# Loading feed-forward weights as fp32 through the hardware queue with a GpSimd cast, and reordering the first and last steps of an attention and feed-forward kernel

## The chip, the cores and the metric

The kernel runs on one core of one Trainium2 chip. The metric is the device time of one execution in microseconds (us). Thirteen executions of the kernel before gave a median of 504.83 us, from 499.0 to 512.78 us.

## The reference

The inputs are `q`, `k` and `v` with 8 batches, 8 heads, 576 rows and a head size of 64, in fp32, and four fp32 weight matrices.

```
scores = q @ k.T / 8                      # per batch and head, 576 x 576
thresh = max(scores, axis=-1) - tau       # tau = 0.02
attn   = softmax(scores where scores >= thresh, else -1e9)
x      = (attn @ v), heads side by side   # 4608 x 512
h      = max(x @ w1, x @ w2, x @ w3)      # 4608 x 768, w1, w2, w3 are 512 x 768
out    = h @ w_out                        # w_out is 768 x 512
```

## The kernel before, in words

**Quads and steps.** Four heads of one batch are a quad; there are 16 quads, two to a batch. A quad takes 9 steps. A step computes the scores of 128 rows of two heads (two tiles of 128x576 in PSUM), their row maxima (VectorE, `nm` and `unused`), two exponentials (ScalarE, `z`), for some tiles a masked multiply (VectorE, `z`), and then two reciprocals (`rs`) and the normalized bf16 tile `P` (GpSimd). A DMA transpose on SyncE's queue turns `P` into a part of `ptq`. There are 144 steps, and each has exactly one `rs` instruction, so that the starts of those are a clock of the steps. Everything is issued through `_Ordered`, whose line 62 is the line that the profile shows for nearly all instructions.

**Other work in the steps.** Each step has two slots for a piece of other work: a transposition of the next quad's `q` or `k` on TensorE (`tp`), a product of `ptq` with `vb` (`o`, evacuated into `xt`), a product of the hidden layer (`hid`, PSUM tile `ph`, for one block `f` of 128 hidden columns and one of the weights), or a product of the output (`po`). The dictionary `plan` has fixed slots for the first two kinds (`TS`, `PA`, `PB`, counted in half steps from the quad's start). Pieces of the feed-forward network wait in the list `todo`, and a free slot takes one; from slot 18*14+`ED` on it takes two. Once both quads of a batch have their `o` products, `o_step` appends the batch's 18 hidden pieces and its output pieces to `todo`. What is left after the last step is done by `rest`.

**Halves.** With two column runs per piece, `hid` issues matmuls of 64 rows that use the upper and the lower half of the array at once, in two rounds that `halves` separates by a gate (a no-op that waits for the first round). When a step has exactly two pieces, `issued` interleaves them in the order of `ARRAY`, so that one piece's second round comes after the other's first. With more than two pieces, or one, a piece's rounds follow each other directly. The last batch is done in two parts with one run of 256 and one of 320 columns, with matmuls of 128 rows.

**Weights.** `weight_loads` makes nine DMAs on GpSimd's queue that cast from fp32 to bf16 on the way: three of 256 columns (`f` 0 and 1), three of 512 columns (`f` 2 to 5), and three pieces of `wo`. They are issued after the steps in `WL`. The hidden pieces of the first batch begin at step 25.

**Order and buffers.** On each engine the instructions of a step follow `ORDER`, where M is the maxima, E the first exponentials, N and K the numerators, R the reciprocal and `P`, and V and A the evacuations of the two pieces. Four buffers hold `z`, six hold `P`, and the loads of `q`, `k` and `v` of a quad have two each and are on SyncE's queue (lines 154 to 174), as are the transposes (line 302) and the stores of the output.

Of the kernel before, what the change touches and what calls it, by code (L numbers as in the profile page):

```python
# [30 lines left out]
ORDER = "V0 A0 R0 K0 V1 M0 M1 A1 N0 K1 N1 E0 E1"  # L31
LAG = dict(M=0, E=0, N=1, K=1)
LATE = 0
ED = 28
WF = (0, 256, 768)
WO = (0, 2, 4, 6)
WL = (14, 16, 18, 24, 26, 28, 31, 33, 35)
LQ = 0
LV = 0
NC = 3  # L40
TS = (9, 11, 13, 15)
PA = 12
PB = 14
# [30 lines left out]
def kernel(  # L74
# [22 lines left out]
    nc = tc.nc  # L97
# [7 lines left out]
    NF = DF // 128  # L105
# [6 lines left out]
    wts = [one.tile([128, 4, DF], BF16, name=f"w{i}") for i in range(3)]  # L112
    wo = one.tile([128, NF, DM], BF16, name="wo")

    def weight_loads():

        for f0, f1 in zip(WF, WF[1:]):
            for w, t in zip((moe_w1, moe_w2, moe_w3), wts):
                yield lambda w=w, t=t, f0=f0, f1=f1: pool.dma_start(
                    out=t[:, :, f0:f1], in_=w[:, f0:f1].rearrange("(ko p) f -> p ko f", p=128))  # L120
        for f0, f1 in zip(WO, WO[1:]):
            yield lambda f0=f0, f1=f1: pool.dma_start(
                out=wo[:, f0:f1, :], in_=moe_w_out[f0 * 128:f1 * 128, :].rearrange("(ko p) m -> p ko m", p=128))
# [240 lines left out]
    def ffn(b, xt, hT, runs, chunks):  # L364


        st = {}
        nr, n = len(runs), runs[0][1] - runs[0][0]

        def hid(f, wi):  # L370
            my = {}

            def start():
                if wi == 0:
                    st["hm"] = hp_.tile([128, nr, n], BF16, name="hm", bufs=3)
                my["hm"], my["ps"] = st["hm"], slot("ph")

            def operands(kc, a):
                c0, c1 = runs[a]
                return (my["ps"][:, a * 512:a * 512 + n],  # L380
                        lambda rows: wts[wi][rows, kc, f * 128:(f + 1) * 128],
                        lambda rows: xt[rows, kc, c0:c1])

            def first():
                start()
                if nr == 1:
                    for kc in range(4):
                        o, w, m = operands(kc, 0)
                        tensor.matmul(o, w(slice(0, 128)), m(slice(0, 128)), start=(kc == 0), stop=(kc == 3))
                else:  # L390
                    my["h"] = halves([[operands(kc, a) for kc in range(4)] for a in range(2)])
                    my["h"][0]()

            def done():
                hm = my["hm"]
                pv = my["ps"].rearrange("p (a u) -> p a u", a=2)[:, :nr, :n]
                if wi == 0:
                    scalar.activation(out=hm, in_=pv, func=AF.Copy)
                else:
                    dst = hm if wi == 1 else \  # L400
                        hT[:, f, runs[0][0]:runs[-1][1]].rearrange("p (a u) -> p a u", a=nr)
                    vector.tensor_tensor(out=dst, in0=pv, in1=hm, op=OP.max)
            return [_Piece(first, (lambda: my["h"][1]()) if nr == 2 else None, done, "V" if wi else "A")]

        rows_out = out[b * S:(b + 1) * S, :].rearrange("(p c) m -> p c m", c=9)

        def outp(c):

            my = {}

            def first():
                my["ps"] = ps = slot("po")
                my["h"] = halves([[(ps[:, 512 * a:512 * a + 512],
                                    lambda rows, a=a, f=f: hT[rows, f, (c + a) * 128:(c + a) * 128 + 128],
                                    lambda rows, f=f: wo[rows, f, :]) for f in range(NF)] for a in range(2)])
                my["h"][0]()

            def done():
                for a in range(2):
                    ob = hp_.tile([128, DM], F32, name="ob", bufs=4)  # L420
                    scalar.activation(out=ob, in_=my["ps"][:, 512 * a:512 * a + 512], func=AF.Copy)
                    nc.sync.dma_start(out=rows_out[:, (0, 2, 1, 3)[c + a]:8:4], in_=ob)
            return [_Piece(first), _Piece(lambda: my["h"][1](), None, done, "A")]

        def ninth():

            my = {}

            def first():
                my["ps"] = ps = slot("po")  # L430
                for f in range(NF):
                    for x in range(2):
                        tensor.matmul(ps[64 * x:64 * x + 64, :256], hT[:, f, 512:S], wo[:, f, 256 * x:256 * x + 256],
                                      start=(f == 0), stop=(f == NF - 1))

            def done():
                ob = hp_.tile([128, DM // 2], F32, name="obr", bufs=2)
                scalar.activation(out=ob, in_=my["ps"][:, :256], func=AF.Copy)
                for x in range(2):
# [3 lines left out]
        return ([pc for f in range(NF) for wi in range(3) for pc in hid(f, wi)],  # L443
                [outp(c) if c < 4 else ninth() for c in chunks])


# [55 lines left out]
    def others(n):  # L502

        ps = []
        for when in (2 * n, 2 * n + 1):
            if when in plan:
                for fn in plan[when]:
                    ps.extend(fn())
            else:
                for _ in range(2 if when >= e + ED else 1):  # L510
                    if todo:
                        ps.append(todo.pop(0))
        return ps

# [27 lines left out]
        return out  # L542

    wl = list(weight_loads())
    for t in vrs:
        for x in range(2):
            vector.memset(t[64 - 64 * x:128 - 64 * x, 2 * x:2 * x + 2, :], 0.0)
# [11 lines left out]
    def step(n, ps):  # L559

        if n + 1 < len(steps):
            g, idx = steps[n + 1]
            c = dict(g=g, idx=idx, z=zz.tile([128, W], F32, name="z"), sm=small.tile([128, 2], F32, name="sm"))

            def scored(r):
                c[r] = scores(Ls[g], idx, r)
            dones = issued(ps, (lambda: scored(0), lambda: scored(1)))
        else:
            c = None
            dones = issued(ps)  # L570
        hist.append(c)
        for what in ORDER.split():
            k, r = what[0], int(what[1])
            if k in "AV":
                if r < len(dones) and dones[r][0] == k:
                    dones[r][1]()
                continue
            x = hist[-1 - LAG.get(k, 0)] if len(hist) > LAG.get(k, 0) else None
            if k == "M" and x:
                x["bias", r] = maximum(x["g"], x["idx"], r, x[r])  # L580
            elif k == "E" and x:
                exponents(x["g"], x["idx"], r, x["z"], x[r], x["bias", r])
            elif k in "NK" and x and masked(x["g"], x["idx"], r) == (k == "K"):
                numerators(x["g"], x["idx"], r, x["z"], x["sm"])
                if r == 1:
                    norm.append(x)
            elif k == "R" and len(norm) > LATE:
                x = norm.pop(0)
                normalized(Ls[x["g"]], x["idx"], x["z"], x["sm"])

    step(-1, [])
    for n, (g, idx) in enumerate(steps):
# [9 lines left out]
        if n % 9 == NC and n // 9 + 1 < NQ:  # L602
            cast_v(Ls[n // 9 + 1])
        step(n, others(n))
        if wl and n in WL:
            wl.pop(0)()
    for _ in range(max(LAG.values()) - 1):
        step(len(steps), [])
    for x in norm:
        normalized(Ls[x["g"]], x["idx"], x["z"], x["sm"])  # L610

    def rest(p):
        for _, done in issued([p]):
            done()
    while todo:
        rest(todo.pop(0))
    for pr in range(2):
        for p in o_step(z_, pr, 2):
            rest(p)
    for p in todo + held:  # L620
        rest(p)
# [1 line left out]
_INS = ['q', 'k', 'v', 'tau', 'moe_w1', 'moe_w2', 'moe_w3', 'moe_w_out']  # L623
_OUTS = [((4608, 512), 'float32')]
# [30 lines left out]
```

## Time and profile before

| | |
|---|---|
| median of 13 executions | 504.83 us |
| profiled execution, its own time | 505.38 us |
| span of its instructions | 503.6 us |
| mean granted TensorE clock | 0.968 |
| TensorE busy | 457.8 us (91%) |
| VectorE busy | 401.9 us (80%) |
| ScalarE busy | 394.3 us (78%) |
| GpSimd busy | 301.3 us (60%) |
| DMA, mean rate | 167 GB/s |

The profiled execution is one execution: its span starts with the first instruction and ends with the last. Busy times count an engine's instructions without its waits. A line of the timeline gives start and length in us, engine, operation, tiles, and, in brackets, the idle time before it and what ended that. The clock row gives the granted TensorE clock in tenths, in 40 slices of 12.6 us.

### The profile page before, as it was taken

What the parts mean: (1) busy time and instruction counts of PE and PEld (TensorE: products, weight loads), DVE (VectorE), ACT (ScalarE), POOL (GpSimd) and SP (SyncE); (2) the same over time, 40 slices, a digit from 0 to 9 for tenths busy, and PEclk for the clock granted to TensorE, in tenths of its full rate; (3) what the DMA queues carried; (4) which work ended last, traced back from release to release, by engine and by line L of the source; (5) the groups of instructions that cost most, each with busy time, mean ns of one, the idle gap of its engine ahead of it and who ended that gap; (6) DMA issues with size and microseconds to landing.
All of it is one profiled execution on the core that took longest, in us unless ns stands there. A gap on an engine that the chain in (4) does not pass through costs nothing.

```text
span 503.6 us, 14001 instructions
## 1 busy us (share of the span) xinstructions
PE 457.8 (91%) x5188; PEld 307.4 (61%) x5188; DVE 401.9 (80%) x996; ACT 394.3 (78%) x814; POOL 301.3 (60%) x413
## 2 busy tenths in 40 slices
PE   7778779389899999999999999999999989999995
PEld 6334347257457675866667675867567665665772
DVE  4998969379499997999798987999799997876450
ACT  4998968279598889889898889889898888864522
POOL 3899877357475747566575757575665876333200
PEclk9897959799899999999999999999999999999999
DMA  7999999989999798978799898979699547842602
GB/s 222 252 216 177 179 233 143 182 167 196 199 194 204 148 191 176 221 167 192 138 213 184 147 189 191 215 156 186 135 237 160 102 83 162 133 85 54 160 12 96
DMA packets 211701, 84.30 MB, mean 167 GB/s; under 512 B 186288, under 2 KB 199344, under 8 KB 211632
## 3 DMA queue, kind: packets, MB, share of 16 engines
q1 hardware_dynamic: 207088, 79.66, 78.8%
q0 software_dynamic: 3984, 3.15, 5.0%
q8 instruction: 41, 0.67, 0.6%
q10 hardware_dynamic: 560, 0.59, 0.4%
q14 instruction: 28, 0.23, 0.2%
HBM read 34.60 MB, written 9.44 MB: 87 GB/s over the span
## 4 chain that ended last, share of the span: by engine, by line
PE 56%; DVE 16%; ACT 12%; DMA 8%; issue 6%; POOL 2%; SPq 0%; ACTq 0%; DVEq 0%; POOLq 0%
PE ph L62 22%; PE sc L62 19%; ACT z L62 9%; PE po L62 9%; DVE unused L62 6%; PE o L62 6%; DVE z L62 4%; DMA w<-in_moe_w_dram 3%; DMA ptq<-P 2%; DVE nm L62 2%; DMA wo<-in_moe_w_out_dram 2%; PE tp L62 2%; ACT ob L62 1%; POOL P L62 1%; DMA qm<-in_q_dram 1%
## 5 line engine op out<-in xcount | busy, mean ns | idle before, releaser
L62 POOL TENSOR_SCALAR P<-z,rs 128x576 bf16<-128x576 f32 x288 | 214.8, 758 | 154.6 <-DVE rs L62 129.1
L62 ACT ACTIVATE z<-sc,nm 128x576 f32<-128x576 f32 x288 | 198.0, 741 | 46.8 <-DVE unused L62 27.1
L62 PE MATMUL sc<-kt,qs 64*128 64x256 f32 (+2 forms) x640 | 190.3, 435 | 10.9 <-ACT z L62 9.7
L62 PE MATMUL sc<-kt,qt 64*128 64x320 f32 (+2 forms) x640 | 190.8, 446 | 8.8 <-ACT z L62 7.8
L62 PE MATMUL ph<-xt,w 64*128 64x288 bf16 (+2 forms) x2160 | 164.5, 285 | 9.7 <-DMA w<-in_moe_w_dram 9.0
L62 DVE TENSOR_SCALAR_CACHE_REDUCE unused<-sc 128x576 bf16<-128x576 f32 x189 | 138.5, 749 | 36.1 <-PE sc L62 35.8
L62 PEld LDWEIGHTS <-w 64*128 64x128 bf16 (+1 forms) x2160 | 127.4, 95 | 42.9 <-issue 12.3
L62 ACT ACTIVATE z<-z 128x576 f32<-128x576 f32 x189 | 129.5, 692 | 0.0
L62 PEld LDWEIGHTS sc<-kt,qs 64*128 64x128 f32 (+1 forms) x640 | 90.2, 181 | 41.7 <-ACT z L62 33.9
L62 PEld LDWEIGHTS sc<-kt,qt 64*128 64x128 f32 (+1 forms) x640 | 91.1, 181 | 32.9 <-ACT z L62 29.3
L62 DVE SCALAR_TENSOR_TENSOR z<-z 128x576 f32<-128x576 f32 x99 | 88.6, 895 | 0.0
L62 DVE TENSOR_REDUCE nm<-sc 128x1 f32<-128x576 f32 x99 | 74.5, 752 | 0.4 <-PE sc L62 0.3
L62 POOL COPY qs<-qt 64x640 f32<-64x640 f32 (+1 forms) x62 | 53.5, 862 | 15.2 <-ACT qt L62 12.1
L62 DVE TENSOR_TENSOR hm<-ph,hm 128x576 bf16<-128x576 f32 (+2 forms) x54 | 37.3, 691 | 29.1 <-PE ph L62 21.9
L62 PE MATMUL po<-wo,hT 64*128 64x512 bf16 (+1 forms) x480 | 54.1, 363 | 2.9 <-DMA wo<-in_moe_w_out_dram 1.9
L62 ACT ACTIVATE hm<-ph 128x576 bf16<-128x576 f32 (+2 forms) x54 | 32.2, 597 | 26.6 <-PE ph L62 26.6
L62 PEld LDWEIGHTS <-hT 64*128 64x128 bf16 (+1 forms) x480 | 26.8, 98 | 26.4 <-issue 8.5
L62 PE MATMUL o<-ptq,vb 128*64 128x64 bf16 (+2 forms) x544 | 41.4, 291 | 1.7 <-DMA ptq<-P 1.7
L62 DVE TENSOR_TENSOR hT<-ph,hm 128x576 bf16<-128x576 f32 (+2 forms) x54 | 37.1, 687 | 5.6 <-PE ph L62 3.9
L62 ACT ACTIVATION_READ_ACCUMULATOR z<-z 128x1 f32 x189 | 39.7, 210 | 0.0
L62 PEld LDWEIGHTS <-vb 128*64 128x64 bf16 x544 | 22.4, 113 | 24.1 <-issue 16.1
L62 DVE RECIPROCAL rs<-sm 128x2 f32<-128x2 f32 x144 | 22.9, 159 | 7.3 <-ACT z L62 2.2
(30 smaller groups left out, 239.9 us busy)
## 6 DMA issues: line engine op xcount, KB each, us to landing
vm<-in_v_dram SPq DMA_DIRECT2D x64, 128.0 KB, 2.9
out_dram<-ob SPq DMA_DIRECT2D x32, 256.0 KB, 2.7
qm<-in_q_dram SPq DMA_DIRECT2D x15, 512.0 KB, 4.4
km<-in_k_dram SPq DMA_DIRECT2D x15, 512.0 KB, 5.8
ptq<-P SPq DMA_TRANSPOSE x144, 3.8
w<-in_moe_w_dram POOLq DMA_DIRECT2D x3, 512.0 KB, 12.6
qm<-in_q_dram SPq DMA_DIRECT2D x16, 64.0 KB, 3.3
vr<-in_v_dram SPq DMA_DIRECT2D x32, 32.0 KB, 2.5
```

What stands on the lines that cost most here:

```text
L62: ins = fn(*a, **kw)
```

## The change

The weights are loaded as fp32 by SyncE's queue in twelve pieces of 512 KB into a buffer `stage` (two buffers), each issued after a step in the new `WL` and turned into bf16 by a GpSimd copy `WC` = 3 steps later. In the first 34 steps the order of work is `ORDER0`, in which the reciprocal and `P` come last instead of near the front, and one more tile may wait for them. The `o` products of the first three quads come two slots (one step) later. The `v` casts of a quad move two steps later (`NC`). In the last batch two hidden products share a PSUM slot and use the halves too. No slot takes two pieces any more (`ED` = 40 lies beyond the last slot), and `rest` issues its pieces in pairs.

```diff
+ORDER0 = "A0 V0 A1 V1 M0 M1 N0 N1 E0 E1 K0 K1 R0"
+N0 = 34
+GE = 3
+PA0 = 14
+PB0 = 16
-ED = 28
-WL = (14, 16, 18, 24, 26, 28, 31, 33, 35)
+ED = 40
+HOLD = 0
+WL = (11, 13, 15, 18, 20, 22, 24, 26, 28, 30, 31, 32)
+WC = 3
-NC = 3
+NC = 5
...
+    stage = ctx.enter_context(tc.tile_pool(name="stage", bufs=2))
...
-        for f0, f1 in zip(WF, WF[1:]):
-            for w, t in zip((moe_w1, moe_w2, moe_w3), wts):
-                yield lambda w=w, t=t, f0=f0, f1=f1: pool.dma_start(
-                    out=t[:, :, f0:f1], in_=w[:, f0:f1].rearrange("(ko p) f -> p ko f", p=128))
+            def load():
+                my["t"] = stage.tile([128, 4 * 256], F32, name="stage")
+                nc.sync.dma_start(out=my["t"].rearrange("p (k f) -> p k f", k=src.shape[1]), in_=src)
+
+            def cast():
+                pool.tensor_copy(out=dst, in_=my["t"].rearrange("p (k f) -> p k f", k=src.shape[1]))
+            return load, cast
+
+        for f in range(0, NF, 2):
+            cols = slice(f * 128, f * 128 + 256)
             for w, t in zip((moe_w1, moe_w2, moe_w3), wts):
+                yield piece(t[:, :, cols], w[:, cols].rearrange("(ko p) f -> p ko f", p=128))
...
-        def hid(f, wi):
+        def hid(*fws):
...
-                if nr == 1:
-                    for kc in range(4):
-                        o, w, m = operands(kc, 0)
-                        tensor.matmul(o, w(slice(0, 128)), m(slice(0, 128)), start=(kc == 0), stop=(kc == 3))
...
+        fws = [(f, wi) for f in range(NF) for wi in range(3)]
+        return ([hid(*fws[x:x + 3 - nr]) for x in range(0, len(fws), 3 - nr)],
...
-        at(18 * g + 18 + PA, lambda g=g: o_step(g, 0))
-        at(18 * g + 18 + PB, lambda g=g: o_step(g, 1))
+        at(18 * g + 18 + (PA0 if g < GE else PA), lambda g=g: o_step(g, 0))
+        at(18 * g + 18 + (PB0 if g < GE else PB), lambda g=g: o_step(g, 1))
...
-        for what in ORDER.split():
+        for what in (ORDER if n >= N0 else ORDER0).split():
...
-            elif k == "R" and len(norm) > LATE:
+            elif k == "R" and len(norm) > (LATE if n >= N0 else 1):
...
-        if wl and n in WL:
-            wl.pop(0)()
+        if n in WL:
+            ahead, behind = wl.pop(0)
+            ahead()
+            casts[n + WC] = behind
+        if n in casts:
+            casts[n]()
...
-    def rest(p):
-        for _, done in issued([p]):
-            done()
+    def rest(ps):
+
+        while ps:
+            for _, done in issued([ps.pop(0) for _ in range(min(2, len(ps)))]):
+                if done:
+                    done()
```

More of the change, by code (lines that the diff above doesn't have):

```diff
@@ L33 @@
 LATE = 0
-ED = 28
-WF = (0, 256, 768)
-WO = (0, 2, 4, 6)
-WL = (14, 16, 18, 24, 26, 28, 31, 33, 35)
+ORDER0 = "A0 V0 A1 V1 M0 M1 N0 N1 E0 E1 K0 K1 R0"
[7 more added lines that the diff above has]
+WC = 3
 LQ = 0
 LV = 0
-NC = 3
+NC = 5
 TS = (9, 11, 13, 15)
@@ L113, with piece @@
     wo = one.tile([128, NF, DM], BF16, name="wo")
+    stage = ctx.enter_context(tc.tile_pool(name="stage", bufs=2))
     def weight_loads():
-        for f0, f1 in zip(WF, WF[1:]):
-            for w, t in zip((moe_w1, moe_w2, moe_w3), wts):
-                yield lambda w=w, t=t, f0=f0, f1=f1: pool.dma_start(
-                    out=t[:, :, f0:f1], in_=w[:, f0:f1].rearrange("(ko p) f -> p ko f", p=128))
-        for f0, f1 in zip(WO, WO[1:]):
-            yield lambda f0=f0, f1=f1: pool.dma_start(
-                out=wo[:, f0:f1, :], in_=moe_w_out[f0 * 128:f1 * 128, :].rearrange("(ko p) m -> p ko m", p=128))
+        def piece(dst, src):
+            my = {}
+            def load():
[6 more added lines that the diff above has]
+            cols = slice(f * 128, f * 128 + 256)
+            for w, t in zip((moe_w1, moe_w2, moe_w3), wts):
+                yield piece(t[:, :, cols], w[:, cols].rearrange("(ko p) f -> p ko f", p=128))
+        for f in range(0, NF, 2):
+            yield piece(wo[:, f:f + 2, :], moe_w_out[f * 128:f * 128 + 256, :].rearrange("(ko p) m -> p ko m", p=128))
     ld = ctx.enter_context(tc.tile_pool(name="ld", bufs=2))
@@ L368, in ffn @@
         nr, n = len(runs), runs[0][1] - runs[0][0]
-        def hid(f, wi):
+        def hid(*fws):
             my = {}
[L373 to L382, printed above, removed]
-            def first():
-                start()
-                if nr == 1:
-                    for kc in range(4):
-                        o, w, m = operands(kc, 0)
-                        tensor.matmul(o, w(slice(0, 128)), m(slice(0, 128)), start=(kc == 0), stop=(kc == 3))
-                else:
-                    my["h"] = halves([[operands(kc, a) for kc in range(4)] for a in range(2)])
-                    my["h"][0]()
-            def done():
[L395 to L403, printed above, removed]
@@ new lines, in hid @@
+            banks = [(f, wi, c) for f, wi in fws for c in runs]
+            def first():
+                my["ps"] = slot("ph")
+                my["h"] = halves([[(my["ps"][:, a * 512:a * 512 + n],
+                                    lambda rows, f=f, wi=wi, kc=kc: wts[wi][rows, kc, f * 128:(f + 1) * 128],
+                                    lambda rows, c=c, kc=kc: xt[rows, kc, c[0]:c[1]]) for kc in range(4)]
+                                  for a, (f, wi, c) in enumerate(banks)])
+                my["h"][0]()
@@ new lines, in done @@
+            def done():
+                pv = my["ps"].rearrange("p (a u) -> p a u", a=2)[:, :, :n]
+                for x, (f, wi) in enumerate(fws):
+                    p = pv[:, x * nr:x * nr + nr]
+                    if wi == 0:
+                        st["hm"] = hp_.tile([128, nr, n], BF16, name="hm", bufs=3)
+                        scalar.activation(out=st["hm"], in_=p, func=AF.Copy)
+                    else:
+                        dst = st["hm"] if wi == 1 else \
+                            hT[:, f, runs[0][0]:runs[-1][1]].rearrange("p (a u) -> p a u", a=nr)
+                        vector.tensor_tensor(out=dst, in0=p, in1=st["hm"], op=OP.max)
@@ L405, in ffn @@
+            return _Piece(first, lambda: my["h"][1](), done, "A" if fws == ((fws[0][0], 0),) else "V")
         rows_out = out[b * S:(b + 1) * S, :].rearrange("(p c) m -> p c m", c=9)
@@ L441, in ninth @@
             return [_Piece(first, None, done, "A")]
-        return ([pc for f in range(NF) for wi in range(3) for pc in hid(f, wi)],
+        fws = [(f, wi) for f in range(NF) for wi in range(3)]
+        return ([hid(*fws[x:x + 3 - nr]) for x in range(0, len(fws), 3 - nr)],
                 [outp(c) if c < 4 else ninth() for c in chunks])
@@ L510, in others @@
                 for _ in range(2 if when >= e + ED else 1):
-                    if todo:
+                    if todo and n >= HOLD:
                         ps.append(todo.pop(0))
@@ L544 @@
     wl = list(weight_loads())
+    casts = {}
     for t in vrs:
@@ L610 @@
         normalized(Ls[x["g"]], x["idx"], x["z"], x["sm"])
-    def rest(p):
-        for _, done in issued([p]):
-            done()
[L615 to L621, printed above, removed]
+    def rest(ps):
[3 more added lines that the diff above has]
+                    done()
+    rest(todo)
+    rest([p for pr in range(2) for p in o_step(z_, pr, 2)])
+    rest(todo + held)
 _INS = ['q', 'k', 'v', 'tau', 'moe_w1', 'moe_w2', 'moe_w3', 'moe_w_out']
```

## The prediction

> **What bounds the kernel now.** I read the slices first, then the waits, then the timelines where a wait is long. The slices show where TensorE is not full.
>
> ```profile
> PE   7778779389899999999999999999999989999995
> ...
> PEclk9897959799899999999999999999999999999999
> DMA  7999999989999798978799898979699547842602
> ```
>
> From slice 12 (138 us) on TensorE is at 9 almost throughout, so there it is the bound: 18 steps (one batch) take 55.8 us, 3.1 us a step. Before that there is a hole, and the clock falls with it. The waits name it:
>
> ```profile
> PE ph L62 <- DMA w<-in_moe_w_dram: 9.0, 2, 7.2
> ...
> PE po L62 <- DMA wo<-in_moe_w_out_dram: 1.9, 1, 1.9
> PE o L62 <- DMA ptq<-P: 1.7, 1, 1.7
> ```
>
> TensorE waits 9.0 us for hidden weights, 1.9 us for output weights, and once for a transpose. Its timeline and VectorE's show the places:
>
> ```profile
> 95.85 3.06 PE L62 MATMUL ph<-xt,w 64*128 64x288 bf16 x24 [7.16 <-DMA w<-in_moe_w_dram]
> ...
> 101.86 2.13 PE L62 MATMUL ph<-xt,w 64*128 64x288 bf16 x32 [1.86 <-DMA w<-in_moe_w_dram]
> ...
> 129.13 3.41 PE L62 MATMUL po<-wo,hT 64*128 64x512 bf16 x16 [1.86 <-DMA wo<-in_moe_w_out_dram]
> ...
> 90.61 0.17 DVE L62 RECIPROCAL rs<-sm 128x2 f32<-128x2 f32 x1
> ...
> 104.22 0.15 DVE L62 RECIPROCAL rs<-sm 128x2 f32<-128x2 f32 x1
> ```
>
> The two reciprocals belong to neighbouring steps, 28 and 29: 13.61 us instead of the 3.2 us of the same place a batch later. The first of these matmul groups also runs slowly (3.06 us for 24; 32 take 2.0 us later).
>
> Busy time by stage (start:end, length, then TensorE, weight loads, VectorE, ScalarE, GpSimd, each with its count, then clock, DMA share, GB/s):
>
> ```profile
> 40.00:60.00 20.00, 16.87 (x130) 9.46 (x130) 18.29 (x48) 17.90 (x38) 18.90 (x26) 0.83 1.12 177
> 60.00:78.00 18.00, 13.63 (x120) 8.01 (x122) 13.49 (x35) 13.02 (x26) 13.56 (x18) 0.72 1.09 216
> ...
> 89.00:103.00 14.00, 5.29 (x52) 3.68 (x54) 3.77 (x11) 4.72 (x9) 3.94 (x7) 0.76 1.29 180
> ...
> 144.50:200.30 55.80, 54.60 (x664) 37.71 (x662) 49.62 (x124) 49.02 (x102) 37.23 (x52) 1.00 0.89 177
> ```
>
> Until the feed-forward work starts, VectorE, GpSimd and the DMAs are all nearly full (18.29 and 18.90 of 20 us, DMA share over 1). At 89 us all engines stand still but the DMAs, which are at 1.29. SyncE's queue shows how a transpose's issue stretches beside the weight DMAs (1.3 us each otherwise):
>
> ```profile
> 82.11 5.72 SPq L302 DMA_TRANSPOSE ptq<-P  x1
> ...
> 89.36 16.66 SPq L302 DMA_TRANSPOSE ptq<-P  x5
> ```
>
> **What the Trainium skill says.** *DMA: Bandwidth & Descriptors*, "SWDGE vs HWDGE vs iDMA": a cast in a DMA is for GpSimd's queue only, so the hardware queue must bring fp32 and somebody else cast; and "Issuing engines are not separate DMA queues": all share 16 engines. The trace agrees: `k` loads issued at 88 us beside the weights land after 11 to 12 us, the median is 5.8. *TensorE: Matmul & The Clock Gate*, Part 1: an idle window of about 3.4 us halves the clock. The trace agrees: 0.76 in the stall. *GPSIMD Engine Reference*, "Key points": GpSimd shares its SBUF interfaces with VectorE. VectorE's masked multiply takes 0.75 to 1.19 us here, so contention is plausible; nothing isolates it.
>
> **The change, part by part.**
>
> 1. *Hidden weights earlier and in the other queue.* The pieces of `f` 2 and 3 are cast after steps 21, 23 and 25; the first hidden product that needs them comes in step 29. Before, the 512-column DMAs went out at 78, 83 and 89 us (steps 24 to 28) and landed after 8.8 to 12.7 us. With four steps (12 us) in hand the stall goes: 13.61 - 3.2 = **-10.4 us**, slow clock included. What is late next: for `f` 4 and 5 the casts are at 27, 29, 31 and the use from step 35, again four steps.
> 2. *Output weights.* Cast at 33 to 35, used from step 38. From `rs` 36 to `rs` 41 the trace has 18.84 us, a batch later 15.33: **-3.5 us**.
> 3. *GpSimd.* Twelve casts are added, nine DMA issues go:
>
> ```profile
> L62 POOL CAST vb<-vm 128x1024 bf16<-128x1024 f32 x16 | 18.1, 1133 | 0.1
> ...
> L62 POOL DMA_DIRECT2D w<-in_moe_w_dram x6 | 4.9, 816 | 0.0
> ```
>
> The `v` cast has the same shape: 12 x 1.133 = 13.6 us, less 4.9 and 2.3 us (three `wo` issues): +6.4 us. Up to step 24 it is five casts (5.7) less three issues (2.4) = +3.3 us, where 40 to 60 us has 1.1 us to spare and 60 to 78 us 4.4. Behind a cast on GpSimd wait `P`, then its transpose and, over the four `z` buffers, ScalarE. Bounds: 0 (spare time covers it) to +3 us; from step 26 a step takes 3.1 us and has room.
> 4. *SyncE's queue and the DMAs.* Twelve loads at 0.5 us of issue each (the `k` loads of the same size take 0.46 to 0.62) = 6 us, five of them (2.5 us) ahead of the transpose of step 17, two even ahead of the first transpose. Two `k` and `q` loads of 512 KB at 9 us land 1.4 us apart, so the twelve cost about 17 us of DMA time; the cast DMAs' packets took 5.0% of the span, 25 us. So the load is not larger, but sits earlier. SyncE runs 3 to 9 us behind `P` in steps 0 to 22; the `o` wait at step 23 (5.66 us between reciprocals) comes from it. The `o` products of quad 1 now come a step later, 2.5 us, which covers the 2.5 us of issue. A load also waits for the cast two pieces back; behind it are the transposes. Bounds: -2.5 (the step-23 wait goes) to +3 us. For 3 and 4 together I take **+2**.
> 5. *`ORDER0`, `NC`, later `o`.* No instruction is added. VectorE's sum per step is the same, and it has no wait for the reciprocal's inputs there. `P` starts up to three VectorE operations (2.4 us) later; two of four `z` buffers' turns cover it. The hidden work starts a step later, in as many slots as it has pieces: 0, bounds -2 to +3, inside the range.
> 6. *The end.* No slot takes two pieces now, so the last steps stay at two and `rest` pairs the remainder. Before:
>
> ```profile
> 450.37 3.59 PE L62 MATMUL ph<-xt,w 64*128 64x288 bf16 x48
> ...
> 456.69 3.68 PE L62 MATMUL ph<-xt,w 64*128 64x288 bf16 x48
> ...
> 471.56 8.03 PE L62 MATMUL ph<-xt,w 128*128 128x256 bf16 x72
> ```
>
> At 2.0 us for 32, 48 should take 3.0: 0.6 + 0.7 too much, because the gates are not interleaved. Two groups of 16 (1.16, 1.42 against 1.0) give 0.6, 36 `po` matmuls about 0.5, four waits of TensorE there (0.25, 0.43, 0.27, 0.40) 1.35: 3.7 us. The last batch's 128-row matmuls take 111 ns for 256 columns; two 64-row ones side by side take 2.0/16 = 125 ns for 288, the same per column: 0. I take **-3**, bounds -5 and +1 (a pair may wait for its slot).
>
> Sum: -10.4 - 3.5 + 2 - 3 = -14.9; the span 503.6 becomes 488.7. The profiled execution took 505.38 us, 1.8 more than its span and 0.55 more than the median; 504.83 - 14.9 = **490.0 us**.
>
> **The rivals.**
>
> - *The DMAs are the bound underneath.* Without the stall the transposes have no 10 us to catch up: at step 26 they ran 16 us late. If the six `P` buffers run out, GpSimd waits and half the gain goes: 490 + 6 = 496. For: DMA share over 1 before the stall. Against: those lags grew beside the cast DMAs, which go.
> - *Slower: the ring of two `stage` buffers.* SyncE holds transposes behind a load that waits for a cast, GpSimd holds `P` behind a cast that waits for its load. It decides when a piece lands more than 16.9/12 = 1.4 us after its cast's turn on average; at 2.2 us it is 26.4 - 16.9 = +9.5, 514 us. For: the transposes' lag of up to 9 us before step 18 nearly uses up the three steps (7.5 us). Against: a late cast delays `P` too, which lets SyncE catch up.
> - *More than I count.* The step-23 wait goes and the tail gives its 5: 503.6 - 10.4 - 3.5 - 2.5 - 5, 482 to 484.
> - *It doesn't do it.* Weights are still late, 503.
>
> **How the numbers follow.** Main case 0.53 (485 to 494 us), DMA-bound 0.20 (494 to 500), more 0.15 (481 to 485), ring 0.08, nothing 0.04. The range 482 to 499 leaves out the ring, nothing, and the ends of two cases. Within 0.5% (2.5 us, about what a measurement of this kernel can tell from no change) of 504.83 lie the last case and a little of the ring: same 0.05, slower 0.07, faster 0.88.
>
> **What would show it.** Right: no wait of `ph` or `po` for weights; steps 28 to 30 at 3.1 us; clock 1.0 from about 85 us; the last steps at 3.1 us and `ph` groups of 32 at 2.0 us after them. Wrong: GpSimd copies of `stage` with idle time ahead by a DMA, ScalarE waiting for `P`, or SyncE's transposes later than before at step 17.

## The result and the profile after

The changed kernel takes 492.47 us (median of 11 runs, 490.01 to 496.43) against 504.56 us before (median of 48 runs, 498.36 to 517.81). The ratio of the two is 0.9806, with a 95% interval from 0.9776 to 0.9837: 1.9% or 9.8 us faster. The prediction was 490.0 us in a range from 482 to 499. The profiled execution of the changed kernel took 489.41 us (span 487.6), a little below the lowest of these; that of before took 505.38 us, about its median. The ratio leaves out the executions that are over 1.5% slower than the fastest of their kernel, which the kernel before has many of and the changed kernel none; the medians of all executions are 12.1 us apart. The two traces are 16.0 us apart where the timed runs are 10 to 12 apart. I use the traces for places and the timed runs for sizes of whole kernels.

The slices of the changed kernel, to hold against those of before (12.2 us each now):

```profile
PE   7787778998999999999999999999999989999995
...
PEclk8978889999999999999999999999999999999999
DMA  7899999999979798959989599969999457754402
```

The hole in TensorE's slice 8 (3 tenths before) is gone, and the clock is at 9 or more from slice 7 on. The DMAs stay at 7 to 9 at the start, as before. Of the waits these bear on the weights:

```profile
ACT z L67 <- POOL P L67: 23.7, 18, 2.3
...
POOL wo L67 <- DMA stage<-in_moe_w_out_dram: 5.0, 1, 5.0
...
PE po L67 <- POOL wo L67: 1.7, 1, 1.7
```

There is no wait of `ph` for weights any more (9.0 us before) and none of `o` for a transpose (1.7 us before). One wait for output weights remains, and it has changed hands: GpSimd waits 5.0 us for a load, and TensorE 1.7 us for GpSimd's cast. ScalarE waits for GpSimd's `P` 23.7 us in all (18.7 before). The timelines of VectorE and TensorE show the places:

```profile
91.40 0.16 DVE L67 RECIPROCAL rs<-sm 128x2 f32<-128x2 f32 x1
...
95.51 0.16 DVE L67 RECIPROCAL rs<-sm 128x2 f32<-128x2 f32 x1
```

```profile
117.08 1.04 PE L67 MATMUL po<-wo,hT 64*128 64x512 bf16 x8 [0.18 <-ACT z L67]
...
119.82 0.61 PE L67 MATMUL po<-wo,hT 64*128 64x512 bf16 x4 [1.70 <-POOL wo L67]
```

The reciprocals of steps 28 and 29 are 4.11 us apart, not 13.61. (Up to step 33 the reciprocal comes later in its step than in the kernel before, so that the start of a step can be compared by it from step 34 on only.) The stages (start:end, length, then TensorE, weight loads, VectorE, ScalarE, GpSimd, each with its count, then clock, DMA share, GB/s):

```profile
40.00:60.00 20.00, 16.67 (x130) 9.53 (x126) 18.49 (x47) 17.08 (x37) 18.05 (x23) 0.83 1.08 213
60.00:78.00 18.00, 13.18 (x131) 7.46 (x131) 16.60 (x44) 14.78 (x30) 17.64 (x21) 0.91 1.07 235
78.00:92.00 14.00, 12.82 (x168) 10.68 (x169) 10.18 (x26) 11.14 (x25) 11.23 (x16) 1.00 1.17 283
...
132.50:188.30 55.80, 54.44 (x662) 38.01 (x660) 49.52 (x122) 48.70 (x102) 36.83 (x51) 1.00 0.93 186
```

From 78 us on the clock is 1.00. In 60 to 78 us GpSimd is now the fullest engine: 17.64 of 18 us, 13.56 before; three of the added casts lie there. The steady batch still takes 55.8 us. So the traces differ in two stretches: up to step 42 the changed kernel gains 11.9 us, from there to step 138 another 0.5, and in the last six steps and after them 3.6. The prediction had 11.9 for the first part (10.4 + 3.5 - 2) and 3 for the end.

At the end, the hidden products come in groups of 32 where the kernel before had 48, and the last batch uses the halves:

```profile
434.76 2.22 PE L67 MATMUL ph<-xt,w 64*128 64x288 bf16 x32
...
456.00 7.59 PE L67 MATMUL ph<-xt,w 64*128 64x256 bf16 x136
...
464.30 0.61 PE L67 MATMUL ph<-xt,w 64*128 64x256 bf16 x8
```

The 144 matmuls of the last two lines take 8.2 us, the 72 of 128 rows before took 8.03: as predicted, nothing is gained there. The last five steps take 14.8 us and not 24.6, because part of the work has moved behind them.

In the traces the sum fits, and that alone says little about its terms. The runs below took it apart.

### The profile page after: what moved, and what is told of

Same layout as the page of the kernel before. It is cut to its first block, busy times and chain, and to the rows that moved or that the text cites. A ratio compares the mean times of both kernels' runs of the same rounds, so it can differ in the third digit from the quotient of the medians.

```text
span 487.6 us, 14288 instructions
## 1 busy us (share of the span) xinstructions
PE 450.1 (92%) x5332; PEld 309.3 (63%) x5332; DVE 403.3 (83%) x996; ACT 393.5 (81%) x814; POOL 311.1 (64%) x416
## 4 chain that ended last, share of the span: by engine, by line
PE 48%; DVE 17%; ACT 16%; issue 8%; POOL 8%; DMA 2%; SPq 0%; ACTq 0%; POOLq 0%; DVEq 0%
PE ph L67 22%; PE sc L67 17%; ACT z L67 13%; PE po L67 7%; DVE unused L67 6%; DVE z L67 4%; POOL P L67 4%; DVE nm L67 3%; PE o L67 2%; POOL qs L67 2%; DVE kt L67 1%; DMA qm<-in_q_dram 1%; ACT ob L67 1%; DVE hm L67 1%; ACT xt L67 1%
## 5 line engine op out<-in xcount | busy, mean ns | idle before, releaser
L67 POOL TENSOR_SCALAR P<-z,rs 128x576 bf16<-128x576 f32 x288 | 221.7, 784 | 120.9 <-DVE rs L67 75.5
L67 PEld LDWEIGHTS <-w 64*128 64x128 bf16 x2304 | 128.0, 94 | 32.4 <-issue 12.4
L67 PEld LDWEIGHTS sc<-kt,qs 64*128 64x128 f32 (+1 forms) x640 | 91.6, 182 | 46.1 <-ACT z L67 33.6
L67 DVE SCALAR_TENSOR_TENSOR z<-z 128x576 f32<-128x576 f32 x99 | 91.0, 919 | 0.0
L67 POOL COPY qs<-qt 64x640 f32<-64x640 f32 (+1 forms) x62 | 49.5, 799 | 11.2 <-ACT qt L67 8.0
L67 PE MATMUL po<-wo,hT 64*128 64x512 bf16 (+1 forms) x480 | 52.6, 357 | 2.1 <-POOL wo L67 1.7
L67 ACT ACTIVATE hm<-ph 128x576 bf16<-128x576 f32 (+2 forms) x54 | 32.2, 597 | 14.3 <-DVE hT L67 7.5
L67 PE MATMUL o<-ptq,vb 128*64 128x64 bf16 (+2 forms) x544 | 39.0, 282 | 0.0
L67 PEld LDWEIGHTS <-vb 128*64 128x64 bf16 x544 | 22.0, 110 | 20.4 <-issue 12.2
```

The costliest lines, as they stand in the source:

```text
L67: ins = fn(*a, **kw)
```

## The experiments

Each kernel was timed in five rounds against the kernel before on the same chip; the experiments ran on four chips, with 6 to 22 executions each. The percentages are the ratio's distance from 1 and 1% is 5.05 us. The intervals stand in the table. "Span" is that of the one profiled execution.

| kernel | median us | ratio to before, 95% interval | span us |
| --- | --- | --- | --- |
| changed kernel | 492.47 | 0.9806 (0.9776 to 0.9837) | 487.6 |
| weights only | 501.0 | 0.9957 (0.9929 to 0.9984) | 497.2 |
| end only | 500.83 | 0.9964 (0.9928 to 1.0001) | 499.0 |
| weights and end, old order | 498.17 | 0.9913 (0.9884 to 0.9942) | 495.2 |
| order only | 504.22 | 1.0012 (0.9976 to 1.0047) | 498.5 |
| changed, old `v` casts | 494.35 | 0.9856 (0.9796 to 0.9916) | 494.5 |
| changed, steady order | 490.78 | 0.9789 (0.9735 to 0.9842) | 488.8 |
| changed, old `o` steps | 495.3 | 0.9874 (0.9820 to 0.9928) | 493.1 |
| weights and end, ScalarE's queue | 500.53 | 0.9961 (0.9936 to 0.9986) | 499.6 |
| changed, last loads earlier | 489.5 | 0.9711 (0.9663 to 0.9760) | 488.1 |
| weights only, last loads earlier | 502.55 | 0.9988 (0.9955 to 1.0022) | 500.7 |
| cast DMAs, earlier | 498.83 | 0.9879 (0.9838 to 0.9920) | 495.0 |
| cast DMAs earlier, with order and end | 491.78 | 0.9782 (0.9732 to 0.9832) | 491.6 |

### The four parts

**Weights only.** The kernel before with the new loads and casts, and nothing else of the change.

```diff
-WL = (14, 16, 18, 24, 26, 28, 31, 33, 35)
+WL = (11, 13, 15, 18, 20, 22, 24, 26, 28, 30, 31, 32)
+WC = 3
...
-                yield lambda w=w, t=t, f0=f0, f1=f1: pool.dma_start(
+                yield piece(t[:, :, cols], w[:, cols].rearrange("(ko p) f -> p ko f", p=128))
```

> The kernel before with the twelve fp32 loads and GpSimd casts alone; its order of work, its o steps and its end stay. My theory (the hole at steps 28 to 29 and the wait for output weights are the gain, casts and loads cost about 2 us): step 29 at 3 to 4 us instead of 13.6, no wait for hidden weights, 10 to 13 us less than before (ratio 0.974 to 0.980), the end as before. If the other order of the first 34 steps is needed to make room for the casts, SyncE's transposes lag more than before at step 17 and less than 8 us is gained. If the ring of two stage buffers holds things up: slower than before.

0.4% faster, 2.2 us, where I expected 10 to 13. Step 29 does what I expected: 3.26 us instead of 13.61. But steps 36 to 41 take 22.87 us, more than the 18.84 of before. The waits of this kernel and GpSimd's timeline:

```profile
POOL wo L63 <- DMA stage<-in_moe_w_out_dram: 7.5, 2, 4.2
...
PE po L63 <- POOL wo L63: 6.0, 1, 6.0
...
POOL w L63 <- DMA stage<-in_moe_w_dram: 5.3, 3, 2.5
```

```profile
115.53 1.04 POOL L63 CAST wo<-stage 128x1024 bf16<-128x1024 f32 x1 [3.29 <-DMA stage<-in_moe_w_out_dram]
...
122.20 1.04 POOL L63 CAST wo<-stage 128x1024 bf16<-128x1024 f32 x1 [4.20 <-DMA stage<-in_moe_w_out_dram]
```

Five of the ten casts after the first two wait for their loads, 12.8 us in all, and GpSimd's queue stands still behind each. The last one lets TensorE wait 6.0 us. The loads are not slow (4.1 to 6.1 us from issue to landing); they are issued late. The last one goes out 14.3 us after the reciprocal of its step, because SyncE takes its queue in order, and in that queue stand transposes that are themselves 4 to 7 us behind `P`. The two `stage` buffers are not what holds them: no load goes out less than 5 us after the cast that frees its buffer. In the traces this kernel is 6.0 us ahead of the kernel before at step 138, more than the timed 2.2.

**End only.** The kernel before with products in halves in the last batch, `ED` = 40 and pairs in `rest`.

```diff
-ED = 28
+ED = 40
...
-        def hid(f, wi):
+        def hid(*fws):
...
-    def rest(p):
+    def rest(ps):
```

> The kernel before with the new end alone (hidden products of the last batch as halves, steps stay at two pieces, remainder in pairs); weights come as before. My theory: nothing changes before step 138, the last six steps and what follows take 3 to 4 us less (ratio 0.992 to 0.994). If the last batch's gain in the changed kernel came from its state at step 138 and not from these edits: 0, within 0.3%.

0.4% faster, 1.8 us, an interval that just reaches 0; in the trace, the time from step 138 to the end is 57.28 us before, 53.98 here and 53.69 in the changed kernel. The gain of 3.3 to 3.6 us at the end comes from these edits and not from the state at step 138. All the traces agree: from step 138 on, the nine kernels with the new end take 53.6 to 54.4 us, the five with the old one 56.9 to 57.6.

Up to step 138 the engines of this kernel run the instructions of the kernel before, so its trace is a second execution of that code and shows how much one trace can tell. At step 138 it is 1.3 us ahead of the first. Single places differ more: step 29 takes 11.50 us and not 13.61, step 23 takes 2.11 and not 5.66, and steps 36 to 41 take 21.94 and not 18.84. Its waits for weights were 9.0 and 1.9 us in the first trace and are here

```profile
PE ph L62 <- DMA w<-in_moe_w_dram: 7.0, 2, 4.4
...
PE po L62 <- DMA wo<-in_moe_w_out_dram: 5.2, 1, 5.2
```

Going by this pair, a single trace gives the length of one early stage to about 3 us. The sums are closer here, but they can differ by more: the timed executions of the kernel before spread over 19 us.

**Weights and end, with the old order.** The changed kernel with `ORDER`, the `o` steps and the `v` casts as before.

```diff
-N0 = 34
-GE = 3
+N0 = 0
+GE = 0
...
-NC = 5
+NC = 3
```

> The changed kernel with the steady order of work from the first step on, o steps and v casts at their old steps: new weights and new end only. My theory (the order of the first 34 steps is worth nothing by itself): within 2 us of the changed kernel, 490 to 495. If the order carries a part of the gain, because GpSimd is nearly full in steps 10 to 24 and the order sets when P can start: 3 us or more slower than the changed kernel, with the wait for a transpose at step 23 back.

0.9% faster: about the sum of the two kernels above (0.4 and 0.4). It is 1.1% or 5.4 us behind the changed kernel, and the intervals do not meet. The expectation of "within 2 us" fails; the second one holds in size, but not in its mechanism: step 23 is short here (2.1 us), and `po` waits 6.4 us for the output weights. Up to the last batch this is the code of the weights-only kernel in a second execution, and steps 36 to 41 take 23.03 us, against 22.87 there.

**Order only.** The kernel before with `ORDER0`, the later `o` steps and the later `v` casts; cast DMAs as before.

```diff
+N0 = 34
+GE = 3
...
-NC = 3
+NC = 5
...
+        at(18 * g + 18 + (PA0 if g < GE else PA), lambda g=g: o_step(g, 0))
```

> The kernel before with the other order of the first 34 steps, later o steps of the first three quads and later v casts; weights by cast DMAs on GpSimd's queue as before. My theory: the step-23 wait shrinks, the hidden work starts one step later, so the wait for weights shrinks by up to a step: 0 to 3 us less (ratio 0.994 to 1.0). If the order is worth a good part of the change's 12 us: over 4 us less.

No change that can be measured: 0.1% slower with an interval on both sides of 1. (Its profiled execution, with a span of 498.5 us, lies near the lowest of its times.) Step 29 still takes 12.9 us. So the order is worth nothing measurable beside the old weights and 5.4 us beside the new ones. Beside the new ones the trace shows where: at steps 36 to 41, which take 17.93 us with the order and 23.03 without, as `po` waits 1.7 us and not 6.4 for its weights. Why nothing is left beside the old weights is not shown. It is not that the hole takes up what the order saved before it: by the starts of the exponentials, this kernel's trace is 1.3 us ahead of the kernel before at step 28 and 3.4 at step 34.

### Which part of the order

**The `v` casts back** at their old steps in the changed kernel:

```diff
-NC = 5
+NC = 3
```

> The changed kernel with the v casts back at their old steps (NC 3). Weights, end, first order and later o steps stay. Theory A (what the order adds is room on SyncE's queue, and the v loads' place beside the first transposes is a good part of it): the transposes of steps 0 to 5 lag 6 us behind P again, more of the stage casts wait for their load, 2 to 4 us slower than the changed kernel (ratio to before 0.985 to 0.989). Theory B (the reciprocals' later place or the later o steps carry it): within 1 us of the changed kernel.

2.5 us slower than the changed kernel (0.9856), though the intervals overlap; in the trace it is 7.0 us behind at step 138. SyncE's queue of this kernel and then of the changed one:

```profile
21.21 4.20 SPq L320 DMA_TRANSPOSE ptq<-P  x2
25.50 1.87 SPq L188 DMA_DIRECT2D vm<-in_v_dram  x3
27.47 1.69 SPq L320 DMA_TRANSPOSE ptq<-P  x1
29.20 0.58 SPq L188 DMA_DIRECT2D vm<-in_v_dram  x1
```

```profile
21.53 7.18 SPq L320 DMA_TRANSPOSE ptq<-P  x4
...
34.74 1.62 SPq L188 DMA_DIRECT2D vm<-in_v_dram  x2
```

The `v` loads follow their casts: with the cast two steps earlier they stand ahead of the third transpose, with the later one behind the sixth. The transposes of steps 3 to 7 and 11 to 17 stand 1.4 to 4.7 us further behind `P` than in the changed kernel, and loads that stand behind a transpose are later too: the third piece of weights goes out at 57.55 us here and at 54.85 in the changed kernel, and six of the casts begin within 0.06 us of their load's landing; in the changed kernel one does.

**The steady order from step 0** in the changed kernel:

```diff
-N0 = 34
+N0 = 0
```

> The changed kernel with the steady order of work from step 0 (the reciprocals in third place, one step earlier); later o steps and v casts stay. Theory B1 (the first order carries the extra gain: P a step later relative to VectorE, transposes less behind): 4 to 6 us slower than the changed kernel (ratio to before 0.989 to 0.992). Theory A: 1 to 2 us slower.

0.9789 against 0.9806: no difference. `ORDER0` itself does nothing that these runs can show. With it the first reciprocal comes 2.0 us later and that of step 33 0.2 us later, but this is its later place in the step: the exponentials of step 22 start 0.5 us apart in the two kernels.

**The `o` steps back** in the changed kernel:

```diff
-GE = 3
+GE = 0
```

> The changed kernel with the o steps of the first three quads back a step earlier; first order and v casts stay. Theory B2 (the o products needed transposes that had not landed, and the feed-forward work started a step too early for its output weights): the wait at step 23 is back and the wait of po for wo grows from 1.7 to 4 us or more, 2 to 5 us slower than the changed kernel. Theories A and B1: within 1 us.

3.4 us slower than the changed kernel (0.9874; the intervals overlap by a little), 5.6 us in the trace. The `o` products come a step too early at step 23 (6.67 us between reciprocals instead of 2.50), which is nearly made up by step 37. What stays is this wait on TensorE:

```profile
122.20 3.41 PE L67 MATMUL po<-wo,hT 64*128 64x512 bf16 x14 [5.48 <-POOL wo L67]
```

Feed-forward work that starts a step earlier comes to its output weights a step earlier. In this execution the load of the last piece, issued at the same time as in the changed kernel (112.79 and 113.18 us), also took 8.3 us instead of 5.5. The three parts taken out one by one cost 0.5, -0.2 and 0.7%, together 1.0%: about the 1.1% between the changed kernel and the one with the old order. As the interval of each ratio is 0.5 to 0.6% to either side, this agreement is no proof that the parts add; that the order is worth 1.1% is shown, its division among the three is not.

### Is it the queue, the time of issue or the way of casting?

**ScalarE's queue.** The kernel with weights, end and old order, its loads issued from ScalarE.

```diff
-                nc.sync.dma_start(out=my["t"]...
+                nc.scalar.dma_start(out=my["t"]...
```

> New weights and new end with the old order throughout, as the earlier kernel without the order, but the twelve fp32 loads are issued from ScalarE's queue and not from SyncE's. If the loads come late because they stand on SyncE's queue behind transposes that wait for P (half of that kernel's stage casts began 0.05 us after their load had landed): no cast waits for its load, po does not wait for wo (6.4 us there), and the time comes to within 2 us of the changed kernel, ratio to before 0.978 to 0.985. If the DMA engines themselves are the limit, the loads land as late as before: 0.989 to 0.993. ScalarE pays about 0.5 us an issue, 6 us in all, of which most should lie in its idle time.

`po` no longer waits for its weights, as expected, and yet the kernel is 2.4 us slower than the same one on SyncE's queue (0.9961 against 0.9913, intervals that just touch), outside both ranges that I had named. I had counted 0.5 us an issue. The issue takes 0.38 us; the cost is in standing before it, as ScalarE's timeline shows:

```profile
79.23 0.37 ACTq L130 DMA_DIRECT2D stage<-in_moe_w_dram  x1
79.65 0.68 ACT L67 ACTIVATE z<-z 128x576 f32<-128x576 f32 x1 [4.52 <-issue]
...
96.05 0.39 ACTq L130 DMA_DIRECT2D stage<-in_moe_w_dram  x1
96.49 1.37 ACT L67 ACTIVATE z<-sc,nm 128x576 f32<-128x576 f32 x2 [1.95 <-POOL w L67]
```

A load needs its `stage` buffer, so it waits for the cast two pieces back; the last five begin 0.02 to 0.04 us after that cast ends. On ScalarE the exponentials stand behind that wait. Before two of the earlier loads ScalarE stood 4.0 and 4.5 us, with no release that the waits name. The semaphore records of the trace name it: the loads and transposes of both queues share eight completion semaphores, and these two loads (at 54.23 and 79.23 us) go out 0.07 us after SyncE's last DMA on the same semaphore has landed, a transpose at 54.17 and a `v` load at 79.17 us. Three more, at 59.79, 69.95 and 84.64 us, follow such a landing by 0.10 us or less. So these loads left SyncE's queue and still waited for its DMAs, and this run does not show what a free queue would give. The Trainium skill (*DMA: Bandwidth & Descriptors*, "Issuing engines are not separate DMA queues") says that issuing from another engine saves only the time that it takes to initiate the DMA. This run agrees that little is to be had, and adds that the wait ahead of the issue moves with it.

**The last six loads earlier** in the changed kernel, one to two steps:

```diff
-WL = (11, 13, 15, 18, 20, 22, 24, 26, 28, 30, 31, 32)
+WL = (11, 13, 15, 18, 20, 22, 23, 25, 27, 28, 29, 30)
```

> The changed kernel with its last six loads (and casts) one to two steps earlier: after steps 23, 25, 27, 28, 29 and 30 and not 24, 26, 28, 30, 31 and 32, so that the last load of output weights stands ahead of the next quad's v, q and k loads on SyncE's queue. If the wait for that load is what steps 36 to 41 still lose: the load goes out near 106 us and not at 113, the 5.0 us wait of GpSimd and the 1.7 us wait of po go, 2 to 3 us less than the changed kernel (ratio to before 0.974 to 0.978). If earlier loads only make the transposes and P later: within 1 us of the changed kernel or slower.

The wait that is left in the changed kernel is explained by SyncE's queue there:

```profile
112.03 0.54 SPq L174 DMA_DIRECT2D km<-in_k_dram  x1
112.62 0.47 SPq L179 DMA_DIRECT2D km<-in_k_dram  x1
113.18 0.41 SPq L130 DMA_DIRECT2D stage<-in_moe_w_out_dram  x1
113.64 13.72 SPq L320 DMA_TRANSPOSE ptq<-P  x7
```

Between the second and the third load of output weights stand ten loads of the next quads and a transpose. With the earlier steps none of the loads does, the third goes out at 105.33 us, and `po` starts without a wait for `wo`:

```profile
120.03 1.59 PE L67 MATMUL po<-wo,hT 64*128 64x512 bf16 x12 [0.20 <-ACT z L67]
```

This kernel has the lowest median of the study: 489.5 us, ratio 0.9711, with an interval that does not meet that of the changed kernel (but meets those of two others in the table). Its profiled execution does not show the gain (span 488.1 against 487.6): the step with the wait, 37 to 38, is 1.7 us shorter, but 34 to 35 is 1.8 us longer, and the four `w` and `wo` casts of steps 26 to 31 begin 0.05 us after their load. So the cause of the wait is settled. The timed gain is 4.8 us by the ratios and 3.0 by the medians, where 2 to 3 were expected; no trace shows where it comes from.

**The same six loads earlier, weights only.** The same `WL` in the first kernel of the study.

> The kernel before with the new weights alone, as in the first experiment, and the same six loads earlier. If the 6.0 us wait of po for the output weights is what that experiment lost against the changed kernel: 4 to 6 us less than it, ratio to before 0.984 to 0.988, without the new order. If the later o steps and v casts are needed for other reasons: little change, 0.994 to 0.997.

Not faster: 0.9988 against 0.9957. TensorE's `po` waits no longer, but its scores do. From the timelines of TensorE and GpSimd:

```profile
117.78 0.90 PE L63 MATMUL sc<-kt,qs 64*128 64x320 f32 x1 [6.88 <-POOL qs L63]
```

```profile
113.92 1.04 POOL L63 CAST wo<-stage 128x1024 bf16<-128x1024 f32 x1 [4.66 <-DMA stage<-in_moe_w_out_dram]
114.94 1.47 POOL L63 TENSOR_SCALAR P<-z,rs 128x576 bf16<-128x576 f32 x2
116.47 1.26 POOL L63 COPY qs<-qt 64x512 f32<-64x512 f32 x2
```

The second `wo` load still stands behind the next quad's `v` loads here (SyncE issues them until 106.51 us): it goes out at 108.03 and lands at 113.87. Its cast has moved forward on GpSimd's queue, ahead of the copy of `qs` that the next scores need. A cast that waits 4.66 us for its data holds `P` and `qs` behind it, and TensorE stands 6.88 us. Here, moving the load and its cast to earlier steps did not help, because the queue did not let the load out much earlier. My explanation of the first experiment ("the 6.0 us wait of `po` is what it lost") falls: with that wait gone the time is no better. The late load is still there, and the wait for it shows up where its cast now stands.

**Cast DMAs, only earlier.** The kernel before with its nine DMAs on GpSimd's queue issued two to six steps earlier. There is no fp32 load and no cast on GpSimd.

```diff
-WL = (14, 16, 18, 24, 26, 28, 31, 33, 35)
+WL = (11, 13, 15, 18, 20, 22, 27, 29, 31)
```

> The kernel before with its nine cast DMAs on GpSimd's queue issued two to six steps earlier (after steps 11, 13, 15, 18, 20, 22, 27, 29 and 31 and not 14, 16, 18, 24, 26, 28, 31, 33 and 35). If only the time of issue matters: no wait at step 29 and 8 to 12 us less than before. If it is the cast DMAs themselves (8.8 to 12.7 us to land, transposes late beside them): they land no faster, the transposes lag more in steps 15 to 30, and the gain is under half of that, or none.

1.2% faster, 6.1 us, by the ratio; by the medians of this kernel and of the kernel before on that chip (502.83) it is 4.0 us. So one line gives between a third and three fifths of the whole change, less than the 8 to 12 us expected, and more than the weights part by itself (0.9957, an interval that does not meet this one). No wait for weights is left anywhere. The Trainium skill's advice (*DMA: Bandwidth & Descriptors*, "Rules for kernel authors") to issue early and wait late holds here. What it costs is at step 23, on TensorE's timeline:

```profile
76.21 2.05 PE L62 MATMUL o<-ptq,vb 128*64 128x512 bf16 x14 [5.37 <-DMA ptq<-P]
```

The transposes of steps 17 to 22 run 10 to 12 us behind `P` beside the cast DMAs (9 us at most there before), so `o` waits 5.37 us where it waited 1.65.

**The same, with the order and the end of the changed kernel.** All of the change but the weights' path.

```diff
-WL = (14, 16, 18, 24, 26, 28, 31, 33, 35)
+WL = (11, 13, 15, 18, 20, 22, 27, 29, 31)
...
+N0 = 34
+GE = 3
...
-NC = 3
+NC = 5
...
-ED = 28
+ED = 40
...
```

> Everything of the change but the weights' path: first order, later o steps and v casts, new end, and the weights still as nine cast DMAs on GpSimd's queue, issued early as in the experiment before (after steps 11 to 31). If the time of issue and the o steps are what counts, and not the fp32 loads with GpSimd casts: no wait at step 29, the 5.4 us wait for a transpose at step 23 shrinks to 2 to 3, and the time is within 3 us of the changed kernel, ratio to before 0.977 to 0.985. If the fp32 loads and casts are needed, because transposes beside cast DMAs stay 10 us behind: the wait at step 23 stays and the ratio is 0.985 or more.

0.9782: not to be told from the changed kernel's 0.9806, though the wait at step 23 or 24 has only shrunk to 4.3 us and not to 2 to 3. Its trace is 3.4 us behind that of the changed kernel at step 138: it loses 5.8 at step 24, where `o` still waits for a transpose, and gains some back at step 38, where `po` does not wait:

```profile
77.55 2.05 PE L67 MATMUL o<-ptq,vb 128*64 128x512 bf16 x14 [4.27 <-DMA ptq<-P]
```

So, to within the half per cent of this interval, the fp32 loads and GpSimd's casts are not needed for the gain. They keep the transposes closer to `P` (0 to 6 us behind in the changed kernel, up to 12 here) and pay for it with casts that wait for loads.

## Why the prediction was right

The mechanism that the forecast leaned on is there: the hole is gone and the end is shorter. The forecast sum of -14.9 us fits the traces (16.0 apart) and is too large for the timed runs (9.8 by the ratio, 12.1 by the medians). Term by term, from the traces:

- **The hole at step 29** (-10.4): -10.35 with the new weights alone (13.61 to 3.26 us), -9.5 in the changed kernel; against the second trace of the old code (11.50) -8.2 and -7.4. Right, but for its cause I named earlier *and* another queue. The kernel with cast DMAs loses the hole just as well (3.26 us) when they are issued earlier; it is the time of issue.
- **Output weights** (-3.5): wrong with the new weights alone: steps 36 to 41 take 22.87 and 23.03 us in two traces, against 18.84 and 21.94 in the two of the old code. In the changed kernel they take 17.93, which is 0.9 to 4.0 us shorter, but by the order's doing. The step that failed is "Cast at 33 to 35, used from step 38": I took the steps in `WL` as the times of issue. SyncE's queue decides them. The last load went out 9.1 us after its step's reciprocal in the changed kernel and 14.3 us with the weights alone.
- **GpSimd and SyncE** (+2): with the weights alone +0.5 us by step 22 and -1.3 by step 23 (+1.6 against the second trace of the old code, which has no long step 23). That is no more than traces of one code differ by, so the spare time that I counted was enough for the casts up to there. Their cost comes later, and as waits of casts for loads, not as their own duration.
- **Order, `v` casts, later `o`** (0, bounds -2 to +3): 0 by itself, and -5.4 us beside the new weights, outside the bounds. I costed it on its own instructions and on the trace of before. What the traces show of it lies on SyncE's queue and at the output weights: `v` loads off the path of the first transposes, and output weights needed a step later.
- **The end** (-3): -3.3 and -3.6 in the traces, -1.8 in the timed runs (0 to -3.6). Right, and so is its zero for the last batch's halves.

The early part came out at 11.9 us (10.7 against the second trace of the old code) because the order gave about what the output weights failed to give. That these two errors cancel is luck. The forecast was right in its result and in its two main terms, and two of the others were wrong in opposite directions.

Of its signs of being right, `ph` has no wait for weights, the clock is 1.00 from 78 us and the last steps take 3.0 us each; `po` keeps a wait of 1.7 us. Two of its signs of being wrong are there in small: one cast on GpSimd waits for its load, and ScalarE waits longer for `P` (23.7 us, 18.7 before). The third is not: the transpose of step 17 stands 4.6 us behind `P`, 9.2 before. One reading was too narrow: the idle window that it names fits the clock in the stall (0.76 in 89 to 103 us), but in 60 to 78 us of the kernel before the clock was lower still (0.72) although the longest idle stretch of TensorE there was 1.7 us. What lowered it there stays open.

Of the rivals, the ring of two `stage` buffers is there by half. Casts do wait for their loads, 12.8 / 12 = 1.07 us a piece with the weights alone and 5.0 / 12 = 0.42 in the changed kernel, below its point of decision of 1.4 us. But no load on SyncE's queue waits for a cast: in the changed kernel each goes out 2.0 us or more after the cast that frees its buffer. Only on ScalarE's queue did the ring close. And the mean is the wrong measure: with 0.9 us a piece (10.8 us in all) the weights-only kernel with earlier loads lost its whole gain, since one of these waits stood ahead of `qs`. The DMA-bound rival is refuted for the changed kernel: its transposes are at most 6 us behind `P` in the first 42 steps, and `P` never waits for one. "More than I count" had 481 to 485 us, below every execution of the changed kernel.

## What to carry to other kernels

When a DMA is late, first try to issue it earlier on the queue that it has; here one line gave between a third and three fifths of what the whole change gave. A step in a list is not a time of issue: count what stands ahead of the load on its queue, and what stands behind the instruction that will wait for it. And a part that is worth nothing by itself may be worth half of the change beside another part, so price the parts against the trace that they will meet, not only against the one at hand. Last, look at two traces of the same code before reading a stage from one: here they differ by over 3 us in single stages.

## What the runs showed of the hardware

The landing time of a cast DMA varies between kernels, and these traces don't tie it to the time of issue. The six for hidden weights land 5.7 to 12.7 us after issue in the kernel before (median 8.4) and 6.5 to 9.1 (median 7.4) in the end-only kernel, which issues them after the same steps. Issued two to six steps earlier they take 5.3 to 9.3 (median 6.7) and, with the order and the end, 5.3 to 12.0 us (median 7.3). The fp32 loads of 512 KB land after 3.9 to 5.6 us in the changed kernel. The issue of a load costs 0.38 us on ScalarE and 0.4 to 0.5 on SyncE at best, a transpose 1.3; next to a wait of 4 us ahead of it, the issue itself is small.
